# Attention output kept in four interleaved runs of tokens, and the token order put back on the way out of PSUM

## The chip, the cores and the metric

The kernel runs on one core of a Trainium2 chip. The metric is the time of one execution on the device in microseconds; lower is better. Before the change it takes 340.39 us (median of 3 runs, 340.26 to 340.43).

## The reference

Three stages follow each other on 1152 tokens (2 batches of 576), each of width 512. The kernel computes all of it in float32, most matmuls as three products of high and low parts (`float32r`).

```python
# 1. linear attention, 8 heads of 64, 128 random features, per batch
phi(x) = exp(h - max(h)) / sqrt(m),  h = x @ omega.T - |x|^2 / 2
num = phi(q) @ (phi(k).T @ v);  den = phi(q) @ sum(phi(k)) + 1e-6
x = (num / den) as [1152 tokens, 512]
# 2. MLP
h = x @ w_in                     # [512, 2048]
x = (h * sigmoid(1.702 * h)) @ w_out
# 3. top-1 mixture of 8 experts with a capacity of 288 tokens each
e = argmax(x @ w_gate);  gate = softmax(x @ w_gate)[e]
out = gate * (relu(x @ w1[e]) @ w2[e])     # tokens past the capacity stay 0
```

## The kernel before

**Attention.** Rows of q, k and v are loaded so that partition n holds the tokens 4n to 4n+3 of a head (n below 128; `JF` is 4), 512 of a batch's 576 tokens; the other 64 tokens are loaded apart, two heads one above the other. Everything up to the normalised result is done for each j = 0 to 3 by itself: the matmul with the features (`pj`), the exponentials on ACT (`kp`, `qp`), phi(k).T @ v (`kvp`), the transposes of phi(q) (`t`, copied to `qt`), the numerators (`nps`) and the division on DVE (`xr`). `do_X(b, p, u)` then turns `xr` by four transposes into a PSUM bank `xps` of 128 x 512, feature by (j, n). `x_out` copies the bank twice: ACT rounds it into `x_hi` (line 398), DVE subtracts that from the bank into `x_lo` (line 399). `x_hi` and `x_lo` have the shape [128, 4, 1152], feature by feature chunk and token, in the order of the tokens; token 4n+j is the element 4n+j, so the bank's unbroken elements go to every fourth place. There are 8 such outputs. `do_Xm(b, p)` does the same for the 64 other tokens, with a bank of 2 chunks x 64 tokens whose order is already that of the tokens; there are 4 of these.

**PSUM.** Small results take the banks of `mbank`, which hands out two single banks, L and M, by turns (later M alone). The next user of a bank waits until the last reader of the one before is done. `t`, `nps`, `xps`, and the gate's `wt_ps`, `wg_ps` and `wp_ps` share them. `tp` and `h_ps` have two banks, `pj` and the MLP's `y` three and one.

**First MLP.** The tokens are taken in four groups G of 288 (`GS`), 16 blocks m of 128 hidden features. `do_h(G, m)` makes 12 matmuls of 288 columns (4 feature chunks c, three products each, `mm3`, lines 98 to 100): weights stationary, `x_hi` or `x_lo` of the group's tokens moving. ACT computes the activation, and `do_y` adds up four output banks of 288 tokens. Groups 0, 1 and 3 are interleaved, with a lag of 3 and 5 blocks; group 2 comes after them. For groups 1 and 3 no second product is made here, only the logits (`do_lg`, with weights folded by `do_wt`, `do_wg` and `do_wp`), since their tokens are outside the two experts computed ahead. After the last block of groups 0 and 2 `do_y` copies the four banks over `x_hi` and `x_lo` (lines 645 and 646). The weights are decoded block by block on DVE (lines 236 to 242), ACT (`win0h` and so on, line 248) and POOL (`win0l`, line 249), in four tiles of [128, 4, 512] for each matrix, where block m of `w_in` takes columns 128(m % 4) on of each chunk.

**Gate and experts.** `do_logits(G)` multiplies `x_hi` and `x_lo` with the gate for G = 0 and 2, copies the result from PSUM (`lgy`, line 726; for G = 1 and 3 `do_lg` has made `lgt`, line 659), transposes it by 96 tokens, and DVE adds the parts (`lg`, line 739). `do_pos` counts tokens of each expert in order of the tokens. `pick_slot` picks an expert for group 0 and one for group 2; its weights are loaded (`eraw`) and split (`eh`, `el`). `do_h2` and `do_y2` are the expert's two products, 8 blocks each, 12 matmuls of 288 columns a block. `do_z_out` copies the four result banks to `z`, by turns on DVE and ACT (lines 879 and 881); `z_rows` transposes 96 tokens at a time, and the rows are masked, scaled and written out. Loops for tokens that are left follow; with these inputs they are not entered.

**Order of the work.** Attention is written out as 40 steps with lags; what remains of it after the last step is put, with a higher priority, between the first slots of the MLP, which begin at about 87 us. The layer that lays out the instructions then gives each engine its own queue, in order, and puts in the waits. In the time between 87 and 110 us the queue of TensorE therefore holds matmuls of attention and of the MLP by turns.

Of the kernel before, what the change touches and what calls it, by code (L numbers as in the profile page):

```python
# [35 lines left out]
def linear_attention__moe__top1_moe_kernel(  # L36
# [14 lines left out]
    nc = tc.nc  # L51
# [12 lines left out]
    TJ = GS // TT  # L64
    JF = S // 128
    SF = JF * 128
    NU = 18
    NP = NG * E
    VW = D + 1
# [123 lines left out]

    x_hi = xp.tile([128, KD, NT], F32R, name="x_hi")
    x_lo = xp.tile([128, KD, NT], F32R, name="x_lo")
    W = {}
    def w_pair(pool, kind, i):
        t = [pool.tile([128, 4, 512], F32R, tag=f"w{kind}{i}{s}", name=f"w{kind}{i}{s}") for s in "hl"]  # L200
# [200 lines left out]
    def do_X(b, p, u):  # L401

        xr = xrs.pop((b, p, u))
        ps = mbank("xps")
        for j in range(JF):
            nc.tensor.transpose(ps[:, j * 128:(j + 1) * 128], xr[:, j], ident)
        hi, lo = (t[:, 2 * p + u, b * S:b * S + SF].rearrange("p (n j) -> p j n", j=JF)
                  for t in (x_hi, x_lo))
        x_out(hi, lo, ps.rearrange("p (j n) -> p j n", j=JF))

    def do_Xm(b, p):
        ps = mbank("xps")
        for u in range(2):
            nc.tensor.matmul(ps[:, u * 64:(u + 1) * 64], xms[p][:, u], fold, start=True, stop=True)
        hi, lo = (t[:, 2 * p:2 * p + 2, b * S + SF:(b + 1) * S] for t in (x_hi, x_lo))
        x_out(hi, lo, ps[:, :128].rearrange("p (u n) -> p u n", u=2))

    npre = len(P["dec"])
    wseq = [(kd, m) for m in range(NF) for kd in ("in", "out")]
# [189 lines left out]
        return [gp.tile([128, GS], F32R, tag=tag, name=tag, bufs=2) for tag in ("ghi", "glo")]  # L609

    def do_h(G, m, full=False):
        tk = slice(G * GS, G * GS + GS)
        hi, lo = w_in(m)
        ps = bank("A", "h_ps")
        for c in range(KD):
            mm3(ps[:, :GS], hi[:, c], lo[:, c], x_hi[:, c, tk], x_lo[:, c, tk],
                c == 0, c == KD - 1)
        if G % 2 and not full:
            g1 = gp.tile([128, GS], F32, tag="g1", name="g1", bufs=5)
            mark["a"] = nc.scalar.activation(g1, ps[:, :GS], ACTF.Gelu_apprx_sigmoid)  # L620
            gs[G, m] = g1
            return
        ghi, glo = parts_tile(G != 0)
        nc.scalar.activation(ghi, ps[:, :GS], ACTF.Gelu_apprx_sigmoid)  # L624
        g32 = gp.tile([128, GS], F32, tag="g1", name="g32", bufs=5)
        mark["a"] = nc.scalar.activation(g32, ps[:, :GS], ACTF.Gelu_apprx_sigmoid)  # L626
        mark["v"] = nc.vector.tensor_tensor(glo, g32, ghi.bitcast(F32), ALU.subtract)  # L627
        gs[G, m] = (ghi, glo)
# [4 lines left out]
    def do_y(G, m):  # L633
        if m == 0:
            yps[G] = y_banks()
        ghi, glo = gs.pop((G, m))
        hi, lo = w_out(m)
        for c in range(KD):
            dc = slice(c * 128, c * 128 + 128)
            mm3(yps[G][c][:, :GS], hi[:, dc], lo[:, dc], ghi, glo, m == 0, m == NF - 1)  # L640
        if m == NF - 1:
            for c in range(KD):
                sl = (slice(None), c, slice(G * GS, G * GS + GS))
                y = yps[G][c][:, :GS]
                nc.scalar.copy(x_hi[sl], y)
                nc.vector.tensor_tensor(x_lo[sl], y, x_hi[sl].bitcast(F32), ALU.subtract)

    def do_lg(G, m):


        i = G - 1 + m % 2
        if i in lgq:
            run_lg()
        lgq[i] = (m, gs.pop((G, m)))
        if len(lgq) == 4 or (G, m) == (3, NF - 1):
            run_lg()
        if (G, m) == (3, NF - 1):
            held_t.append(gp.tile([128, GS], F32, tag="g1", name="lgt", bufs=5))
            nc.scalar.copy(held_t[0], held.pop()[:, :GS])

    lgq, held_t, now = {}, [], [0]

# [53 lines left out]
    def do_logits(G):  # L716
        if G % 2 == 0:
            ps = mbank("lg_ps")
            for c in range(KD):
                tk = slice(G * GS, G * GS + GS)  # L720
                nc.tensor.matmul(ps[:2 * E, :GS], wg[:, c].rearrange("p a e -> p (a e)"), x_hi[:, c, tk],
                                 start=(c == 0), stop=False)
                nc.tensor.matmul(ps[:E, :GS], wg[:, c, 0], x_lo[:, c, tk],
                                 start=False, stop=(c == KD - 1))
            t = gp.tile([2 * E, GS], F32, tag="g1", name="lgy", bufs=5)
            nc.scalar.copy(t, ps[:2 * E, :GS])
            n = 2 * E
        else:
            n = 64 if G == 1 else 128
            t = held_t[0]  # L730
# [124 lines left out]
    def do_h2(key, m, wt, tok):  # L855
# [1 line left out]
        hi, lo = wt[m // 4]  # L857
        fc = slice((m % 4) * 128, (m % 4) * 128 + 128)
        for c in range(KD):
            mm3(ps[:, :GS], hi[:, c, fc], lo[:, c, fc], x_hi[:, c, tok], x_lo[:, c, tok],  # L860
                c == 0, c == KD - 1)
        hhi, hlo = parts_tile(True)
        nc.scalar.activation(hhi, ps[:, :GS], ACTF.Relu)
# [12 lines left out]
    def do_z_out(key, z):  # L876
        for c in range(KD):
            if c % 2:
                nc.scalar.copy(z[:, c], zps[key][c][:, :GS])
            else:  # L880
                nc.vector.tensor_copy(z[:, c], zps[key][c][:, :GS])

    def z_rows(z, j):
        ps = mbank("zt_ps")
# [106 lines left out]
    slot(NSL + NF2 + 3, lambda: slot_rows(0, 1))  # L991
    slot(NSL + NF2 + 4, lambda: slot_rows(0, 2))

    def tokens(G):
        return slice(G * GS, (G + 1) * GS)

    for n in range(NSL + 2 * NF2 + 2):
        now[0] = n
        if n < NSL:
# [23 lines left out]
    with tc.If(n_left > 0):  # L1023
# [23 lines left out]
        with tc.For_i(0, n_left):  # L1047
# [19 lines left out]
                split_e(wt, i, "x")  # L1067
            for m in range(NF2 + 1):
                if m < NF2:
                    do_h2("x", m, wt, ds(gv * GS, GS))  # L1070
                if m:
                    do_y2("x", m - 1, wt)
            z, base = scratch(0)
# [38 lines left out]
```

## Time and profile before

| | |
|---|---|
| median of 3 runs | 340.39 us (340.26 to 340.43) |
| the profiled execution | 339.27 us, of it 337.5 from the first to the last instruction (the span) |
| mean granted TensorE clock | 0.996 |
| TensorE busy | 318.7 us, 94% |
| VectorE (DVE) busy | 182.9 us, 54% |
| ScalarE (ACT) busy | 172.4 us, 51% |
| GpSimd (POOL) busy | 60.4 us, 18% |

A group of instructions is written as line, engine, operation, output<-inputs, shapes and count, then busy us and mean ns of one, then the idle time of the engine just before them and what ended it. PE is TensorE's matmul. The ends of matmuls are modelled: matmuls are pipelined, and one row lasts longer than the distance to the next. In the chain of waits each piece is start us, length us and what.

### The profile page before, as it was taken

How to read it: one execution, taken by the hardware profiler on the slowest of the kernel's cores; microseconds unless marked ns; L12 is line 12 of the kernel's file. 1: busy time of each engine (PE TensorE's matmuls, PEld its weight loads, DVE VectorE, ACT ScalarE, POOL GpSimd, SP SyncE). 2: the span in 40 equal slices, each digit the busy share in tenths (PEclk: the TensorE clock that was granted, in tenths of full speed). 3: DMA queues.
4: the chain of work that ended last, by engine and by line, in shares of the span. 5: the costliest groups of instructions: out<-in, count | busy, mean ns of one | idle time of the engine just before them, and what ended most of it. 6: DMA issues, size and time to landing. Idle time of an engine off the chain costs nothing.

```text
span 337.5 us, 6635 instructions
## 1 busy us (share of the span) xinstructions
PE 318.7 (94%) x2569; PEld 304.3 (90%) x2569; DVE 182.9 (54%) x438; ACT 172.4 (51%) x445; POOL 60.4 (18%) x83
## 2 busy tenths in 40 slices
PE   5999999989997999999999999999999999999991
PEld 4999998889896999999999999989999999998990
DVE  5678797887578775444446403117434123568322
ACT  2788888879834454444444434233634233165312
POOL 3110311122003444443443410000000001010000
PEclk9999999999999999999999999999999999999998
DMA  6999541401030545435441000523400000383202
GB/s 173 296 328 271 166 134 62 127 15 50 0 105 25 186 130 172 151 122 170 124 135 64 0 2 0 156 95 94 135 23 0 2 1 2 110 271 119 72 0 80
DMA packets 29079, 35.19 MB, mean 104 GB/s; under 512 B 5360, under 2 KB 23792, under 8 KB 29040
## 3 DMA queue, kind: packets, MB, share of 16 engines
q1 hardware_dynamic: 29040, 34.69, 33.0%
q8 instruction: 22, 0.36, 0.5%
q14 instruction: 17, 0.14, 0.1%
HBM read 32.33 MB, written 2.36 MB: 103 GB/s over the span
## 4 chain that ended last, share of the span: by engine, by line
PE 82%; ACT 6%; DVE 5%; DMA 4%; issue 1%; POOL 0%; SPq 0%; ACTq 0%; DVEq 0%
PE h_ps L98 12%; PE h_ps L99 12%; PE h_ps L100 12%; PE y L98 7%; PE y L100 7%; PE y L99 7%; PE kvp L339 4%; PE nps L364 3%; DMA eraw<-in_moe_w_dram 3%; PE tp L282 2%; PE pj L98 2%; ACT x_hi L398 2%; PE t L353 2%; PE pj L99 2%; PE pj L100 2%; PE wt_ps L492 2%
## 5 line engine op out<-in xcount | busy, mean ns | idle before, releaser
L627 DVE TENSOR_TENSOR glo<-g,ghi 128x288 fp32r<-128x288 f32 x27 | 12.9, 478 | 38.7 <-ACT g L626 38.7
L236 DVE TENSOR_SCALAR wf<-wraw 128x512 int32<-128x512 int32 x32 | 16.2, 512 | 26.9 <-POOL win2l L249 10.8
L620 ACT ACTIVATE g<-h_ps 128x288 f32<-128x288 f32 x32 | 13.2, 412 | 29.4 <-PE h_ps L100 24.5
L308 DVE TENSOR_REDUCE nb<-pj 128x4 f32<-128x512 f32 (+1 forms) x40 | 25.1, 631 | 3.9 <-PE pj L100 3.5
L851 DVE TENSOR_TENSOR el<-eraw,eh 128x1024 fp32r<-128x1024 f32 x16 | 19.5, 1222 | 12.0 <-ACT eh L850 12.0
L98 PE MATMUL pj<-om_hi,xh 128*128 128x256 f32 x72 | 24.6, 341 | 1.0 <-ACT qp L321 1.0
L242 DVE SCALAR_TENSOR_TENSOR wf<-wraw,wf 128x512 int32<-128x512 int32 x32 | 25.0, 784 | 0.5
L624 ACT ACTIVATE ghi<-h_ps 128x288 fp32r<-128x288 f32 x27 | 11.1, 412 | 24.5 <-PE h_ps L100 23.9
L850 ACT CAST eh<-eraw 128x1024 fp32r<-128x1024 f32 x16 | 16.7, 1049 | 13.4 <-PE h_ps L99 7.3
L321 ACT ACTIVATE qp<-pj,nb 128x128 f32<-128x128 f32 x72 | 21.8, 389 | 0.7 <-DVE nb L308 0.5
L239 DVE SCALAR_TENSOR_TENSOR wf<-wraw,wf 128x512 int32<-128x512 int32 x32 | 21.9, 691 | 0.2
L99 PE MATMUL pj<-om_lo,xh 128*128 128x256 f32 x72 | 21.7, 301 | 0.0
L321 ACT ACTIVATE kp<-pj,nb 128x128 f32<-128x128 f32 x72 | 21.6, 394 | 0.0
L100 PE MATMUL pj<-om_hi,xl 128*128 128x256 f32 x72 | 21.4, 298 | 0.0
L285 ACT CAST xh<-tp 128x256 fp32r<-128x256 f32 (+1 forms) x40 | 14.7, 369 | 11.7 <-PE tp L282 11.7
L98 PE MATMUL h_ps<-x_hi,win0h 128*128 128x288 f32 x64 | 20.1, 314 | 0.0
L100 PE MATMUL h_ps<-x_hi,win0l 128*128 128x288 f32 x64 | 19.2, 300 | 0.5 <-POOL win0l L249 0.5
L339 PE MATMUL kvp<-vt,kp 128*128 128x65 f32 (+1 forms) x144 | 19.7, 269 | 0.0
L98 PE MATMUL h_ps<-x_hi,win3h 128*128 128x288 f32 x64 | 19.6, 306 | 0.0
L98 PE MATMUL h_ps<-x_hi,win2h 128*128 128x288 f32 x64 | 19.6, 306 | 0.0
L98 PE MATMUL h_ps<-x_hi,win1h 128*128 128x288 f32 x64 | 19.4, 303 | 0.0
L98 PE MATMUL h_ps<-x_hi,eh 128*128 128x288 f32 x64 | 19.2, 300 | 0.0
(246 smaller groups left out, 1080.5 us busy)
## 6 DMA issues: line engine op xcount, KB each, us to landing
wraw<-in_moe_w_in_dram SPq DMA_DIRECT2D x16, 512.0 KB, 4.3
wraw<-in_moe_w_out_dram SPq DMA_DIRECT2D x16, 512.0 KB, 3.6
eraw<-in_moe_w_dram SPq DMA_DIRECT2D x16, 512.0 KB, 4.7
qk_raw<-in_v_dram SPq DMA_DIRECT2D x4, 512.0 KB, 5.2
qk_raw<-in_q_dram SPq DMA_DIRECT2D x4, 512.0 KB, 5.2
qk_raw<-in_k_dram SPq DMA_DIRECT2D x3, 512.0 KB, 5.1
out_dram<-zer SPq DMA_DIRECT2D x2, 576.0 KB, 6.3
out_dram<-base SPq DMA_DIRECT2D x6, 192.0 KB, 3.0
```

What stands on the lines that cost most here:

```text
L98: nc.tensor.matmul(o, lh, rh, start=start, stop=False)
L99: nc.tensor.matmul(o, lh, rl, start=False, stop=False)
L100: nc.tensor.matmul(o, ll, rh, start=False, stop=stop)
L236: nc.vector.tensor_scalar(f, high, 3, 0x3FFFFFF8, ALU.logical_shift_left, ALU.bitwise_and)
L239: nc.vector.scalar_tensor_tensor(f, high, -0x40000000, f, ALU.bitwise_and, ALU.bitwise_or)
L242: nc.vector.scalar_tensor_tensor(f, low, 29, f, ALU.logical_shift_right, ALU.bitwise_or)
L285: nc.scalar.copy(xh[:, :n], tp[:, :n])
L308: mark["M", s] = nc.vector.tensor_reduce(nb[:, :nj], pj[:, :nj * M].rearrange("p (a m) -> p a m", m=M), AX, ALU.min)
L321: nc.scalar.activation(t[:, i], pj[:, i * M:(i + 1) * M], ACTF.Exp, bias=nb[:, i:i + 1], scale=-1.0)
L339: nc.tensor.matmul(ps[:, o:o + n], kp[:, i], vts[p][:, u, c0:c0 + n], start=(f == 0), stop=(f == NU - 1))
L850: nc.scalar.copy(hi, tv)
L851: nc.vector.tensor_tensor(lo, tv, hi.bitcast(F32), ALU.subtract)
```

## The change

`x_hi` and `x_lo` become [128, 4, 4, 288]: token 4i+j lies at (j, i). `do_X` now writes four runs of 128 elements. `do_Xm` writes its 64 tokens to 16 places in each of four runs, so that its inner step is 288 elements. All matmuls on a group of tokens read four runs of 72 in place of one of 288; their results have the order (j, i) in PSUM. `do_y` writes its banks back to `x_hi` and `x_lo` in that order. Where a result leaves PSUM for good (`lgy`, `lgt`, `z`), the copy reads PSUM in steps of 72 elements and writes the tokens in their own order; nothing behind these copies changes. The number of instructions is the same, and no DMA is touched.

```diff
+    NI = NT // JF
+    GI = GS // JF
+    BI = S // JF
...
-    x_hi = xp.tile([128, KD, NT], F32R, name="x_hi")
-    x_lo = xp.tile([128, KD, NT], F32R, name="x_lo")
+    def tokens(G):
+        return slice(G * GI, (G + 1) * GI)
+    def in_order(t):
+        return t.rearrange("p (j i) -> p i j", j=JF)
+    def rows_of(t):
+        return t.rearrange("p (i j) -> p i j", j=JF)
+    x_hi = xp.tile([128, KD, JF, NI], F32R, name="x_hi")
+    x_lo = xp.tile([128, KD, JF, NI], F32R, name="x_lo")
...
@@ do_X
-        hi, lo = (t[:, 2 * p + u, b * S:b * S + SF].rearrange("p (n j) -> p j n", j=JF)
-                  for t in (x_hi, x_lo))
+        hi, lo = (t[:, 2 * p + u, :, b * BI:b * BI + 128] for t in (x_hi, x_lo))
@@ do_Xm
-        hi, lo = (t[:, 2 * p:2 * p + 2, b * S + SF:(b + 1) * S] for t in (x_hi, x_lo))
-        x_out(hi, lo, ps[:, :128].rearrange("p (u n) -> p u n", u=2))
+        hi, lo = (t[:, 2 * p:2 * p + 2, :, b * BI + 128:(b + 1) * BI].rearrange("p u j i -> p u i j")
+                  for t in (x_hi, x_lo))
+        x_out(hi, lo, ps[:, :128].rearrange("p (u i j) -> p u i j", u=2, j=JF))
@@ do_h (do_h2 and do_logits alike)
-            mm3(ps[:, :GS], hi[:, c], lo[:, c], x_hi[:, c, tk], x_lo[:, c, tk],
+            mm3(ps[:, :GS], hi[:, c], lo[:, c], x_hi[:, c, :, tk], x_lo[:, c, :, tk],
@@ do_y
-                sl = (slice(None), c, slice(G * GS, G * GS + GS))
-                y = yps[G][c][:, :GS]
+                sl = (slice(None), c, slice(None), tokens(G))
+                y = yps[G][c][:, :GS].rearrange("p (j i) -> p j i", j=JF)
@@ do_lg
-            nc.scalar.copy(held_t[0], held.pop()[:, :GS])
+            nc.scalar.copy(rows_of(held_t[0]), in_order(held.pop()[:, :GS]))
@@ do_logits
-            nc.scalar.copy(t, ps[:2 * E, :GS])
+            nc.scalar.copy(rows_of(t), in_order(ps[:2 * E, :GS]))
@@ do_z_out
-                nc.scalar.copy(z[:, c], zps[key][c][:, :GS])
+                nc.scalar.copy(rows_of(z[:, c]), in_order(zps[key][c][:, :GS]))
             else:
-                nc.vector.tensor_copy(z[:, c], zps[key][c][:, :GS])
+                nc.vector.tensor_copy(rows_of(z[:, c]), in_order(zps[key][c][:, :GS]))
```

## Rows read from the trace of the kernel before

**Rows 1.** The page: engines' busy time, and the chain that ended last by engine

```profile
PE 318.7 (94%) x2569; PEld 304.3 (90%) x2569; DVE 182.9 (54%) x438; ACT 172.4 (51%) x445; POOL 60.4 (18%) x83
...
PE 82%; ACT 6%; DVE 5%; DMA 4%; issue 1%; POOL 0%; SPq 0%; ACTq 0%; DVEq 0%
```

**Rows 2.** TensorE by stretch: length, busy (instructions), granted clock, DMA; one sum of five

```profile
87.00:90.00 3.00, 2.26 (x20) 1.00 0.00 0
sum 15.00, PE 13.09; mean PE 2.62
...
65.50:71.00 5.50, 3.83 (x41) 1.00 0.24 84
101.50:108.00 6.50, 4.11 (x29) 1.00 0.03 13
30.00:110.00 80.00, 73.75 (x618) 1.00 0.27 84
110.00:304.00 194.00, 193.97 (x1571) 1.00 0.30 93
270.00:280.00 10.00, 10.00 (x77) 1.00 0.00 1
```

**Rows 3.** The chain of waits from 33 to 88 us, pieces of two outputs

```profile
33.64 1.09 ACT x_hi L398
...
34.76 1.10 DVE x_lo L399
...
86.55 1.11 ACT x_hi L398
```

**Rows 4.** TensorE's instructions in order of time, about 35 us

```profile
35.13 0.36 PE L98 MATMUL pj<-om_hi,xh 128*128 128x256 f32 x1
35.92 0.66 PE L353 MATMUL t<-ident,qp 128*128 128x128 f32 x4 [0.42 <-DVE den L382]
```

**Rows 5.** Groups of instructions on DVE and ACT, by shape

```profile
L308 DVE TENSOR_REDUCE nb<-pj 128x4 f32<-128x512 f32 x32 | 21.8, 684 | 1.7 <-PE pj L100 1.3
...
L355 ACT COPY qt<-t 128x512 f32<-128x512 f32 x16 | 9.5, 594 | 4.1 <-PE t L353 3.8
...
L399 DVE TENSOR_TENSOR x_lo<-xps,x_hi 128x512 fp32r<-128x512 f32 x8 | 8.8, 1095 | 7.1 <-ACT x_hi L398 7.0
L398 ACT CAST x_hi<-xps 128x512 fp32r<-128x512 f32 x8 | 8.7, 1089 | 2.9 <-PE xps L406 2.8
...
L384 DVE TENSOR_TENSOR xr<-nps,den 128x256 f32<-128x256 f32 x16 | 6.7, 418 | 0.1
...
L308 DVE TENSOR_REDUCE nb<-pj 128x2 f32<-128x256 f32 x8 | 3.4, 420 | 2.2 <-PE pj L100 2.2
...
L248 ACT CAST win1h<-wf 128x512 fp32r<-128x512 f32 x4 | 2.5, 626 | 2.4 <-DVE wf L242 2.4
...
L881 DVE COPY z<-y 128x288 f32<-128x288 f32 x4 | 1.8, 455 | 3.0 <-PE y L100 3.0
...
L879 ACT COPY z<-y 128x288 f32<-128x288 f32 x4 | 1.5, 399 | 3.9 <-PE y L100 3.9
...
L398 ACT CAST x_hi<-xps 128x128 fp32r<-128x128 f32 x4 | 1.1, 266 | 4.8 <-PE xps L414 4.8
L739 DVE TENSOR_REDUCE lg<-lgr_ps 96x24 f32<-96x48 f32 x4 | 0.8, 202 | 6.0 <-PE lgr_ps L733 6.0
```

**Rows 6.** The chain of waits from 65 to 107 us, pieces of two stretches

```profile
65.48 1.00 ACT x_hi L398
...
67.84 1.44 DVE wf L236
...
103.58 1.29 POOL win0l L249
...
104.90 1.51 DVE wf L236
```

**Rows 7.** The chain of waits about 306 us

```profile
306.51 0.47 DVE z L881
```

More of the change, by code (lines that the diff above doesn't have):

```diff
@@ L611, in do_h @@
     def do_h(G, m, full=False):
-        tk = slice(G * GS, G * GS + GS)
+        tk = tokens(G)
         hi, lo = w_in(m)
@@ L719, in do_logits @@
             for c in range(KD):
-                tk = slice(G * GS, G * GS + GS)
-                nc.tensor.matmul(ps[:2 * E, :GS], wg[:, c].rearrange("p a e -> p (a e)"), x_hi[:, c, tk],
+                tk = tokens(G)
+                nc.tensor.matmul(ps[:2 * E, :GS], wg[:, c].rearrange("p a e -> p (a e)"), x_hi[:, c, :, tk],
                                  start=(c == 0), stop=False)
-                nc.tensor.matmul(ps[:E, :GS], wg[:, c, 0], x_lo[:, c, tk],
+                nc.tensor.matmul(ps[:E, :GS], wg[:, c, 0], x_lo[:, c, :, tk],
                                  start=False, stop=(c == KD - 1))
             t = gp.tile([2 * E, GS], F32, tag="g1", name="lgy", bufs=5)
-            nc.scalar.copy(t, ps[:2 * E, :GS])
+            nc.scalar.copy(rows_of(t), in_order(ps[:2 * E, :GS]))
             n = 2 * E
@@ L859, in do_h2 @@
         for c in range(KD):
-            mm3(ps[:, :GS], hi[:, c, fc], lo[:, c, fc], x_hi[:, c, tok], x_lo[:, c, tok],
+            mm3(ps[:, :GS], hi[:, c, fc], lo[:, c, fc], x_hi[:, c, :, tok], x_lo[:, c, :, tok],
                 c == 0, c == KD - 1)
@@ L992, in linear_attention__moe__top1_moe_kernel @@
     slot(NSL + NF2 + 4, lambda: slot_rows(0, 2))
-    def tokens(G):
-        return slice(G * GS, (G + 1) * GS)
     for n in range(NSL + 2 * NF2 + 2):
@@ L1069, in linear_attention__moe__top1_moe_kernel @@
                 if m < NF2:
-                    do_h2("x", m, wt, ds(gv * GS, GS))
+                    do_h2("x", m, wt, ds(gv * GI, GI))
                 if m:
```

## The prediction, made before the result was known

> **What bounds the kernel now.** I read the page first, then the time line of TensorE by stage, then groups of instructions by shape, then the chain of waits. The page says that TensorE is busy for 94% of the span and holds 82% of the chain that ended last, with ACT 6% and DVE 5% beside it [rows 1]. So nothing counts that does not move TensorE. The stretches show where it could move: from 110 to 304 us it is busy for 193.97 of 194 us, while from 30 to 110 us, where attention ends and the first MLP sets in, it is busy for 73.75 of 80, so 6.25 us of idleness lie there [rows 2]. Nearly all of that lies right behind the eight outputs of attention (`do_X`): five short stretches that each follow one of them hold 15.00 - 13.09 = 1.91 us, the stretch from 65.5 to 71 us holds 1.67 and the one from 101.5 to 108 us 2.39, together 5.97 of the 6.25 [rows 2]. The clock is granted in full in every one of these rows, so it is no term.
>
> The chain of waits shows the mechanism at 33.64 us: ACT writes `x_hi` for 1.09 us, DVE then writes `x_lo` for 1.10, and only then do four transposes start, since `x_lo` was the last reader of their PSUM bank [rows 3]. On TensorE the transposes start at 35.92, 0.79 us after the matmul before them (the row names `den`, which DVE starts as `x_lo` ends) [rows 4], where matmuls of that shape start about 0.12 us apart. Seven of the eight wide outputs stand in the chain, five of them with both copies, the first at 33.64 and the last of these five at 86.55 [rows 3].
>
> **The change part by part.**
>
> *The eight wide outputs.* Each copies 128x512 from PSUM into every fourth element of `x_hi` (ACT) and `x_lo` (DVE); after it, in four unbroken runs of 128. The strided copies take 1089 and 1095 ns; the same number of elements written unbroken takes ACT 594 ns (`qt`), and a DVE pass over 128x512 of PSUM 684 ns [rows 5]. That runs cost nothing of themselves is seen in `xr`: 256 elements in four runs of 64 take 418 ns, and an unbroken DVE pass over 256 takes 420 [rows 5]. So ACT saves 1089 - 594 = 495 ns and DVE 1095 - 684 = 411, say 0.88 us (0.91 less a little, as the reduction writes little and a subtraction writes all) on each hand-over from bank to bank.
>
> What of it TensorE gets: after the five simple outputs the idle time in front of the waiting instruction is 1.91 us in all, on average 0.38, at most 0.74 (the last, from 87 to 90 us) [rows 2], which is less than 0.88; all of it goes. It is a lower bound, as matmul ends are modelled: at 35.92 the idle time is written as 0.42, while 0.79 - 0.12 = 0.67 us passed without a start [rows 4]. With 0.2 added for each, and no more than 0.88 for one, the five give up to 2.8.
>
> From 65.5 to 71 us the wait is longer: ACT's `x_hi` at 65.48 holds up ACT's next exponentials (TensorE waits for their bank), `x_lo` holds up DVE's decode at 67.84 with its 1.44 us [rows 6], and behind that `xl` and `xm`, for which TensorE waits again. Both queues move up by the saving, so 0.88 of the 1.67 goes; the slow decode instruction remains. From 101.5 to 108 us two outputs stand close together on ACT, and behind them in ACT's queue `win0h`, behind that POOL's `win0l`, DVE's decode, and last a narrow output's matmuls. Two ACT savings, 2 x 0.495 = 0.99 us, reach POOL; its 1.29 us and DVE's 1.51 stay [rows 6]. So 0.98 of the 2.39 goes.
>
> Sum of the gain: 1.91 + 0.88 + 0.98 = 3.77 us (up to 2.8 + 1.86 = 4.7; if the two long stretches give only half, 1.91 + 0.93 = 2.8). What is late next: the other reader of the two small PSUM banks, and in the long stretches POOL. From 110 us TensorE is full, so a stage that begins earlier ends earlier.
>
> *The four narrow outputs* (`do_Xm`) lose: 128 elements went out unbroken in 266 ns [rows 5], and now each goes to another place. By the wide rows a scattered element costs (1089 - 594) / 512 = 0.97 ns more, so 0.12 us on ACT and as much on DVE. Two of the four lie beside full TensorE time; bounds for all: 0 to 0.24 x 4 = 1.0 us. I take 0, since no TensorE wait ends on a narrow copy.
>
> *The MLP matmuls.* The 4 x 16 x 12 + 2 x 8 x 12 = 960 matmuls of `h_ps` and the 16 of the logits now read their moving operand in four runs of 72. No row of this trace has a moving operand in more than one run. The bounds: below, a gain is excluded, since the operand is unbroken today. The nearest row is `xr`, where four runs cost DVE nothing. [...] One scattered element for each break, 3 x 0.97 ns, would be 2.8 us. I take 0, as by `xr`. [...]
>
> *MLP results into `x_hi`* (eight pairs, four runs of 72): 0, as by `xr`.
>
> *Order put back on leaving PSUM.* `lgy`, `lgt` and the eight copies `z` now read PSUM in steps of 72 elements and write unbroken. DVE has a row for that: the logit reduction reads 48 elements, none beside the next, in 202 ns; the two reductions over 512 and 256 give 684 - 420 = 264 ns per 256, 1.03 an element, so 420 - 208 x 1.03 = 206 ns for 48 [rows 5]. The steps cost nothing there. ACT has no such row. Below nothing is excluded, the write being unbroken before and after. Upper bound: 0.97 ns for each element as in the strided writes, 288 x 0.97 = 0.28 us a copy. On the path would be `lgy`, which is ahead of the second expert's load, two `z` of DVE in the first expert's results (the second of them at 306.51 [rows 7]), and the last `z` of ACT, for which the final transposes wait: 4 x 0.28 = 1.1 us. I take 0 for DVE and 0.15 for the two ACT copies together. [...]
>
> *Dependencies.* The tokens of different groups now lie between each other in `x_hi`. If the layer that places waits saw a tile's stretch from first to last element as one, `h_ps` would wait for outputs of other tokens. The decoded weights already lie like that (four runs of 128 in one tile, each read and written by another step), and `win1h` waits only for DVE, never for a matmul [rows 5]. So 0. No DMA is added, moved or changed, and nothing on SP's or POOL's queue.
>
> **Sum.** -3.77 + 0.15 = -3.6 us. The profiled execution took 339.27 us (span 337.5), so it would take 335.7; the median of the runs shown is 340.39, 1.1 above it, so I say 336.8 us for the median. About 0.2%, 0.7 us, is what a measurement of this kernel can tell from no change.
>
> **Rivals.**
>
> 1. *The matmuls pay for their runs* (the slower side). Place: every `h_ps` matmul from 87 us on, where TensorE has no slack [rows 2]. The point of balance is 3.6 / 976 = 3.7 ns for each, 2.8% of a step; from 4.4 ns it is measurably slower. [...] For it: nothing else in this trace reads so. Against it: `xr`, and that a break is no new instruction. 0.12.
>
> 2. *The waits are replaced.* The instruction that waited for `x_lo` finds the other bank, an exponential or POOL's 1.3 us in its way, or the instructions come out in another order on the queues, and under 0.7 us arrives: about 340.0. For it: ACT and DVE are busy for most of this stage, and two of the seven stretches have POOL or a slow decode in them [rows 6]. Against it: in five places the chain names both copies [rows 3]. 0.09.
>
> 3. *Stepped PSUM reads are dear on both engines:* 1.1 us instead of 0.15, so 337.7. For it only the size of the strided writes; against it the logit row [rows 5]. [...] 0.09.
>
> **How the numbers follow.** The forecast, gain of 1.5 to 5 us, has 0.70 and a range of its own of 335.3 to 338.9. Rival 3 is faster too. Of rival 2 half is faster by a little, of rival 1 a small part ends level. Faster: 0.70 + 0.09 = 0.79, less 0.02 for what may be lost in both, so 0.77; same 0.10; slower 0.13. The range runs from the upper sum, 340.4 - 4.7 - 0.5 for savings in other gaps, 335.2, to 340.3, where rival 2 ends; the matmul case lies outside.
>
> **What would show it.** The wide `x_hi` copy at about 600 ns and `x_lo` at about 700; if these stay above 1000 ns, the whole forecast falls. TensorE's idle time from 30 to 110 us at about 2.5 us in place of 6.25, with the transposes after the first output waiting for nothing. 77 `h_ps` and `y` matmuls in 10 us of the dense stage, as now; 74 or fewer would be rival 1. `z` on ACT at 399 ns and on DVE at 455 as now [rows 5], or about 680 and 735 for rival 3. A matmul that waits for `x_hi` of another group of tokens would show that the dependencies went wrong.

## The result, and the profile after

The kernel after took 334.49 us (median of 4 runs, 334.21 to 334.96) against 340.32 for the kernel before (4 runs, 339.16 to 340.43): a ratio of 0.984, interval 0.9803 to 0.9877. The forecast was 336.8 us with a range from 335.2 to 340.3. The direction was right; the time came out 2.3 us under the forecast and 0.7 us under the range. Over all runs of this study the kernel after has a median of 334.96 (15 executions) and the kernel before one of 339.81 (44), 4.85 us apart. The two profiled executions are 5.06 us apart: 334.21 with a span of 332.4, and 339.27 with 337.5.

The page of the kernel after, first the engines and then the chain that ended last [rows 1]:

```profile
PE 317.0 (95%) x2569; PEld 303.7 (91%) x2569; DVE 178.7 (54%) x438; ACT 169.4 (51%) x445; POOL 60.3 (18%) x83
...
PE 86%; DMA 5%; ACT 3%; DVE 2%; SPq 1%; issue 1%; POOL 0%; ACTq 0%; DVEq 0%
```

The numbers of instructions are the same. ACT and DVE have lost about half of their share of the chain (6% to 3%, 5% to 2%), and TensorE has taken most of it (82% to 86%). The instructions of every queue stand in the same order in both traces, so nothing was laid out anew. TensorE by stretch (length, busy time and instructions, granted clock, DMA) [rows 2]:

```profile
30.00:110.00 80.00, 77.66 (x658) 1.00 0.31 96
270.00:280.00 10.00, 10.00 (x78) 1.00 0.01 2
```

The idleness between 30 and 110 us fell from 6.25 to 2.34 us (the prediction said about 2.5), and the dense stage is as dense as it was, 78 matmuls in 10 us against 77. Groups of instructions by shape (busy us, mean ns of one, then the idle time before) [rows 5]:

```profile
L411 DVE TENSOR_TENSOR x_lo<-xps,x_hi 128x512 fp32r<-128x512 f32 x8 | 5.5, 692 | 3.6 <-ACT x_hi L410 3.3
L410 ACT CAST x_hi<-xps 128x512 fp32r<-128x512 f32 x8 | 4.7, 591 | 2.9 <-PE xps L418 2.8
...
L893 DVE COPY z<-y 128x288 f32<-128x288 f32 x4 | 1.8, 453 | 3.0 <-PE y L103 3.0
L410 ACT CAST x_hi<-xps 128x128 fp32r<-128x128 f32 x4 | 1.6, 393 | 4.6 <-PE xps L425 4.5
L411 DVE TENSOR_TENSOR x_lo<-xps,x_hi 128x128 fp32r<-128x128 f32 x4 | 1.5, 387 | 0.7 <-ACT x_hi L410 0.7
...
L891 ACT COPY z<-y 128x288 f32<-128x288 f32 x4 | 1.5, 400 | 4.0 <-PE y L103 4.0
```

The wide copies went from 1089 and 1095 ns to 591 and 692, the narrow ones rose from 266 to 393 on ACT (387 on DVE, where step_psum below has the unbroken 280), and the copies that now read PSUM in steps of 72 elements (`z`, 453 and 400 ns) cost what the unbroken ones cost (455 and 399). The matmuls that read four runs of 72 cost nothing more either; here one group of the kernel before and the same one after:

```profile
L98 PE MATMUL h_ps<-x_hi,win1h 128*128 128x288 f32 x64 | 19.4, 303 | 0.0
```

```profile
L101 PE MATMUL h_ps<-x_hi,win1h 128*128 128x288 f32 x64 | 19.4, 303 | 0.0
```

**Where the time came from.** Idle time on TensorE depends on modelled ends; starts do not. So the best ruler is the time from one wide output's four transposes (`xps`, line 406 before, 418 after) to the next one's, and from the eighth to the first transposes of `lgt` in the gate (`lgr_ps`; those of group 0's `lgy` come about 20 us earlier), behind which the distance of the two traces hardly changes. As an example the fourth, the fifth and the gate, on the time line (start, length, engine, line, operation), before and then after:

```profile
64.69 0.60 PE L406 MATMUL xps<-ident,xr 128*128 128x128 f32 x4
78.86 0.60 PE L406 MATMUL xps<-ident,xr 128*128 128x128 f32 x4
...
227.57 0.37 PE L733 MATMUL lgr_ps<-ident,lgt 64*96 64x64 f32 x3
```

```profile
63.13 0.60 PE L418 MATMUL xps<-ident,xr 128*128 128x128 f32 x4
75.73 0.60 PE L418 MATMUL xps<-ident,xr 128*128 128x128 f32 x4
...
222.19 0.37 PE L745 MATMUL lgr_ps<-ident,lgt 64*96 64x64 f32 x3
```

The intervals, in us, each from two such starts (the kernels other than these two are described below; three more of them have their intervals where they are described):

| kernel | 1 to 2 | 2 to 3 | 3 to 4 | 4 to 5 | 5 to 6 | 6 to 7 | 7 to 8 | 8 to gate |
|---|---|---|---|---|---|---|---|---|
| before | 8.00 | 14.10 | 9.58 | 14.17 | 6.95 | 14.03 | 0.84 | 126.89 |
| after | 7.36 | 13.68 | 9.25 | 12.60 | 6.31 | 13.27 | 0.84 | 126.04 |
| after_again | 7.36 | 13.68 | 9.25 | 12.60 | 6.31 | 13.25 | 0.84 | 127.46 |
| after_b | 7.36 | 13.67 | 9.26 | 12.60 | 6.32 | 13.27 | 0.83 | 126.05 |
| step_psum | 7.36 | 13.68 | 9.26 | 12.59 | 6.31 | 13.16 | 0.84 | 126.04 |
| both_slow | 7.96 | 14.13 | 9.58 | 14.15 | 6.91 | 14.10 | 0.84 | 128.25 |
| act_slow | 7.58 | 13.88 | 9.36 | 12.96 | 6.55 | 13.69 | 0.83 | 126.86 |
| dve_slow | 7.51 | 13.75 | 9.25 | 12.62 | 6.43 | 13.56 | 0.83 | 126.08 |
| late_wf | 7.36 | 13.67 | 9.26 | 13.26 | 6.32 | 13.25 | 0.84 | 127.36 |
| late_wf_b | 7.36 | 13.69 | 9.25 | 13.25 | 6.32 | 13.26 | 0.84 | 127.38 |

An interval of one kernel repeats within 0.02 us from execution to execution, but for the last one, of which more below. Before less after: 0.64, 0.42, 0.33, 1.57, 0.64, 0.76, 0 and 0.85, in all 5.21 us. The intervals 1 to 2, 2 to 3, 3 to 4, 5 to 6 and 6 to 7 are the prediction's five simple outputs: 2.79 us. The interval 4 to 5 holds its stretch from 65.5 to 71 us: 1.57. The last one holds its stretch from 101.5 to 108 us: 0.85. The first output is 0.17 us earlier, which is within the spread of its start between executions (more below); with it the gate is 5.38 us earlier; 0.3 of that is lost again by the end, and the spans differ by 5.1.

What is left of TensorE's waits in the kernel after (total us, times, longest):

```profile
PE xps L425 <- DVE xm L406: 1.1, 1, 1.1
...
PE h_ps L103 <- POOL win0l L261: 0.6, 1, 0.6
```

None of them ends on a wide copy any more.

**What the interval 4 to 5 shows.** All engines' time line, first of the kernel before:

```profile
67.71 1.28 POOL L249 TENSOR_TENSOR win0l<-wf,win0h 128x512 fp32r<-128x512 f32 x1 [6.28 <-ACT win0h L248]
67.84 1.44 DVE L236 TENSOR_SCALAR wf<-wraw 128x512 int32<-128x512 int32 x1
...
69.72 0.58 DVE L394 TENSOR_TENSOR xm<-nps,den 64x128 f32<-64x128 f32 x2
69.86 0.33 PE L282 MATMUL tp<-ident,qk_raw 128*128 128x128 f32 x1 [0.58 <-DVE xl L292]
...
70.45 0.64 PE L502 MATMUL wg_ps<-wt,wg_f 128*32 128x128 f32 x16 [0.26 <-DVE xm L394]
```

and then of the kernel after:

```profile
64.44 0.69 DVE L411 TENSOR_TENSOR x_lo<-xps,x_hi 128x512 fp32r<-128x512 f32 x1 [1.26 <-ACT x_hi L410]
65.39 0.43 DVE L248 TENSOR_SCALAR wf<-wraw 128x512 int32<-128x512 int32 x1
65.78 1.28 POOL L261 TENSOR_TENSOR win0l<-wf,win0h 128x512 fp32r<-128x512 f32 x1 [6.17 <-ACT win0h L260]
...
66.27 0.58 DVE L406 TENSOR_TENSOR xm<-nps,den 64x128 f32<-64x128 f32 x2
...
67.32 0.65 PE L514 MATMUL wg_ps<-wt,wg_f 128*32 128x128 f32 x16
```

The reader is to look at two starts. Before, POOL's `win0l` begins at 67.71 and DVE's decode `wf` at 67.84, 0.13 us behind it, and the decode takes 1.44 us: it ends at 69.28, 0.29 after POOL (67.71 + 1.28 = 68.99). After, the decode begins at 65.39, 0.39 ahead of POOL, and takes 0.43 us. The "slow decode instruction" of the prediction was not slow by itself; it stood behind POOL. Of the 32 decodes of this shape the median takes 0.43 us in both traces. How the one instruction holds up the other no run shows. What the trace shows is that the decode ends only behind POOL's instruction, 0.29 us behind it; that this is less than the decode's own 0.43 us is not explained by any run.

One more decode turns over between the two traces. At 46.60 us before, it takes 1.08 us behind POOL's `wout0l` of 46.12; after, it starts with `wout0l` at 44.89 and takes 0.43, and POOL 1.55. TensorE does not gain by it: from its `kvp` matmuls beside the decode to its next transposes 0.67 us pass in both (46.65 to 47.32, 45.42 to 46.09).

### The profile page after: what moved, and what is told of

Its sections match the earlier page's. It is cut to its first block, busy times and chain, and to the rows that moved or that the text cites. A ratio compares the mean times of both kernels' runs of the same rounds, so it can differ in the third digit from the quotient of the medians.

```text
span 332.4 us, 6635 instructions
## 1 busy us (share of the span) xinstructions
PE 317.0 (95%) x2569; PEld 303.7 (91%) x2569; DVE 178.7 (54%) x438; ACT 169.4 (51%) x445; POOL 60.3 (18%) x83
## 3 DMA queue, kind: packets, MB, share of 16 engines
HBM read 32.33 MB, written 2.36 MB: 104 GB/s over the span
## 4 chain that ended last, share of the span: by engine, by line
PE 86%; DMA 5%; ACT 3%; DVE 2%; SPq 1%; issue 1%; POOL 0%; ACTq 0%; DVEq 0%
PE h_ps L101 13%; PE h_ps L102 12%; PE h_ps L103 12%; PE y L101 7%; PE y L102 7%; PE y L103 7%; PE kvp L351 4%; PE nps L376 4%; DMA eraw<-in_moe_w_dram 3%; PE pj L101 2%; PE t L365 2%; PE pj L102 2%; PE pj L103 2%; PE tp L294 2%; PE wt_ps L504 2%; DMA qk_raw<-in_k_dram 2%
## 5 line engine op out<-in xcount | busy, mean ns | idle before, releaser
L248 DVE TENSOR_SCALAR wf<-wraw 128x512 int32<-128x512 int32 x32 | 14.5, 458 | 28.2 <-POOL win2l L261 10.8
```

Of the source, the lines that this page charges most:

```text
L248: nc.vector.tensor_scalar(f, high, 3, 0x3FFFFFF8, ALU.logical_shift_left, ALU.bitwise_and)
```

## The experiments

Two theories stood after the comparison. The first: the copies' length does it all, in two ways, as shorter hand-overs (the 0.88 us a piece of the prediction) and, at one place that TensorE waits for, as an earlier start of the decode that takes it out of POOL's way. The rival: some of the 5 us comes from elsewhere in the change, the new token order (matmuls, dependencies), and the copies give only the predicted 3.8.

**The same kernel again** (after_again, after_b): the kernel after, unchanged.

> The changed kernel once more, as the measure for the other runs. Theory (queue and collision): what the prediction missed is real. Time 334.5 us, 5.5 us under the kernel before; in this second trace the decode instruction that took 1.44 us at 67.84 us takes about 0.43 us again, since it starts ahead of POOL's win0l. Rival (jitter): the first trace was a lucky one; here the decode takes over 1 us, or the difference is about 3.8 us as in the prediction's sum.

Measured: 335.25 us (334.47 to 335.62), ratio 0.9874 (0.985 to 0.9898) against a before of 339.57. The decode took 0.43 us again, at 65.07, with POOL's `win0l` at 65.45.

> The kernel after, unchanged, for a comparison with the late decode within one set of runs. Theory (a sum of stalls, 5.1 to 5.8 us): 334.5 to 335.3 us against a before near 339.8; the decode behind the gating sum (wf, 128x512 int32, near 65 us) takes 0.43 us again and starts ahead of GpSimd's win0l. Second theory, on the spread between executions of one kernel: if TensorE's granted clock falls behind the stall at 99 to 102 us in some executions and not in others, this trace shows either 1.00 in all of 102 to 106 us, or 0.5 there and everything behind it about 1 us later.

Measured: 334.85 us (334.44 to 336.34), ratio 0.9849 (0.982 to 0.9877) against a before of 340.33. So the distance lies between 4.3 and 5.8 us, by the set of runs. The table says why: up to the eighth output the three executions agree in each interval within 0.02 us, and after_again is 1.41 us longer in the last one. Its TensorE there (length, busy, granted clock, DMA), and the same of the kernel after below it:

```profile
98.00:100.00 2.00, 1.43 (x11) 1.00 0.00 0
100.00:102.00 2.00, 0.96 (x7) 0.88 0.00 0
102.00:104.00 2.00, 2.00 (x11) 0.50 0.06 13
104.00:106.00 2.00, 2.00 (x14) 0.77 0.79 249
```

```profile
98.00:100.00 2.00, 1.44 (x11) 1.00 0.00 0
100.00:102.00 2.00, 0.95 (x8) 1.00 0.00 0
102.00:104.00 2.00, 2.00 (x18) 1.00 0.00 0
104.00:106.00 2.00, 2.00 (x17) 1.00 0.79 243
```

After the same idleness (1.43 and 0.96 us busy of 2, against 1.44 and 0.95) the granted clock falls from 1.00 to 0.50 in one execution and stays at 1.00 in the other. It makes 11 matmul records in 2 us instead of 18. Among the profiled executions of this study the fall is in after_again, both_slow, late_wf and late_wf_b, each time behind this same stall, and these are the rows of the table with 1.3 to 1.4 us more in the last interval than their like. This, and the start of the first output (32.51 to 33.58 us in the three executions), is what these traces show of the spread between executions that the timings below carry. What decides whether the clock falls was not found.

**The copies' part alone** (step_psum): the kernel before, whole, with the two wide copies reading PSUM in steps and writing in the order of the tokens, unbroken.

```diff
-        hi, lo = (t[:, 2 * p + u, b * S:b * S + SF].rearrange("p (n j) -> p j n", j=JF)
+        hi, lo = (t[:, 2 * p + u, b * S:b * S + SF].rearrange("p (n j) -> p n j", j=JF)
                   for t in (x_hi, x_lo))
-        x_out(hi, lo, ps.rearrange("p (j n) -> p j n", j=JF))
+        x_out(hi, lo, ps.rearrange("p (j n) -> p n j", j=JF))
```

> The kernel before with one edit: the wide copies write x_hi and x_lo unbroken in the order of the tokens and read PSUM in steps of 128 elements instead. No matmul reads in runs, no result is put back in order. Theory (only the strided SBUF write was dear, a stepped PSUM read is free): wide copies 590 to 700 ns, narrow ones 266 and 278 as before, time within 0.5 us of the changed kernel, 334.0 to 335.0 us. Rival (PSUM steps are dear in long copies): copies near 1.09 us and 340 us. Rival (the layout itself gives part of the gain): 336 us or more with fast copies.

Measured: 334.6 us (333.71 to 336.68), ratio 0.987 (0.984 to 0.99), beside 335.25 for the kernel after in the same set. Its copies by shape:

```profile
L399 DVE TENSOR_TENSOR x_lo<-xps,x_hi 128x512 fp32r<-128x512 f32 x8 | 5.5, 692 | 3.7 <-ACT x_hi L398 3.3
L398 ACT CAST x_hi<-xps 128x512 fp32r<-128x512 f32 x8 | 4.7, 592 | 2.9 <-PE xps L406 2.8
...
L399 DVE TENSOR_TENSOR x_lo<-xps,x_hi 128x128 fp32r<-128x128 f32 x4 | 1.1, 280 | 0.6 <-ACT x_hi L398 0.6
L398 ACT CAST x_hi<-xps 128x128 fp32r<-128x128 f32 x4 | 1.1, 267 | 4.6 <-PE xps L414 4.5
```

Two lines do all that the change does: the step of 128 elements between one read of PSUM and the next costs ACT and DVE nothing (592 and 692 ns, as with unbroken reads in the kernel after), where the step of four on the side of the write had cost 0.4 to 0.5 us (1095 and 1089 ns). The narrow copies stay at 267 and 280 ns, and the interval 6 to 7 is 0.11 us shorter than in the kernel after, the only one in which the two differ by more than 0.02. Neither the new token order nor the work to undo it was needed.

**The new order with slow copies** (both_slow, act_slow, dve_slow): the kernel after, all of it, but the wide copies written element by element, each 288 places from the last; both, only ACT's, only DVE's. Here is both_slow; act_slow and dve_slow do it to the first or the second of the two instructions.

```diff
-        hi, lo = (t[:, 2 * p + u, :, b * BI:b * BI + 128] for t in (x_hi, x_lo))
-        x_out(hi, lo, ps.rearrange("p (j n) -> p j n", j=JF))
+        nc.scalar.copy(x_hi[:, 2 * p + u, :, b * BI:b * BI + 128].rearrange("p j n -> p n j"),
+                       ps.rearrange("p (j n) -> p n j", j=JF))
+        nc.vector.tensor_tensor(x_lo[:, 2 * p + u, :, b * BI:b * BI + 128].rearrange("p j n -> p n j"),
+                                ps.rearrange("p (j n) -> p n j", j=JF),
+                                x_hi[:, 2 * p + u, :, b * BI:b * BI + 128].rearrange("p j n -> p n j").bitcast(F32),
+                                ALU.subtract)
```

> [...] Theory (all of the gain is the wide copies): copies about 1.1 us, time back at 340.3 us, within 0.7 us. Rival (runs in the matmuls or the layout gain or cost something): a time away from that of the kernel before by the size of it; at 3.7 ns a matmul it would be 344 us.

Measured: 339.47 us (338.39 to 341.54), ratio 0.9994 (0.9976 to 1.0011). With copies of 1072 and 1081 ns the whole change is worth nothing, and every interval up to the eighth output is the one of before within 0.07 us. Its time line from 66 us:

```profile
66.74 1.07 DVE L420 TENSOR_TENSOR x_lo<-xps,x_hi 128x512 fp32r<-128x512 f32 x1 [1.65 <-ACT x_hi L419]
67.96 1.28 POOL L261 TENSOR_TENSOR win0l<-wf,win0h 128x512 fp32r<-128x512 f32 x1 [6.28 <-ACT win0h L260]
68.06 1.47 DVE L248 TENSOR_SCALAR wf<-wraw 128x512 int32<-128x512 int32 x1
```

The decode is behind POOL again, and slow again. The rival falls with these two runs: the copies are sufficient (step_psum) and necessary (both_slow).

> The changed kernel with only ACT's wide copy slow (1.09 us), DVE's in runs (0.7). Theory: the five simple stalls come back by what is over after 0.4 us of DVE's saving, about 1.0 us in all; the stretch at 65 us loses 0.5 us, but POOL's win0l moves back with ACT, so the decode still starts ahead of it and stays at 0.43 us; the stretch at 100 us loses 1.0 us. About 337.0 us. Rival (no collision theory, the savings simply add): half of the gain lost, 337.4 us, without a telling decode row.

Measured: 336.87 us (336.36 to 338.22), ratio 0.9934 (0.9909 to 0.996). The rival's 337.4 is within the spread, so the time does not choose; the decode took 0.43 us, as the theory said, and against the kernel after the five simple intervals lose 1.19 us (1.0 expected), 4 to 5 loses 0.36 (0.5) and the last 0.82 (1.0).

> The changed kernel with only DVE's wide copy slow (1.09 us), ACT's in runs (0.6). Theory: the simple stalls come back by about 0.7 us; the decode behind x_lo at 65 us now starts 0.4 us later, after POOL's win0l has begun, and takes about 1.4 us, so 1.0 us more comes back there, with up to 0.4 at 100 us: 336.5 to 337.0 us. Rival (the decode's 1.44 us belongs to itself and not to POOL): the decode stays at 0.43 us and the time is about 335.5 us.

Measured: 335.3 us (333.77 to 335.72), ratio 0.9848 (0.9814 to 0.9882). The decode of 1.4 us, on which the 336.5 to 337.0 rested, did not come:

```profile
65.19 1.05 DVE L420 TENSOR_TENSOR x_lo<-xps,x_hi 128x512 fp32r<-128x512 f32 x1 [1.26 <-ACT x_hi L419]
66.49 0.43 DVE L248 TENSOR_SCALAR wf<-wraw 128x512 int32<-128x512 int32 x1
66.53 1.54 POOL L261 TENSOR_TENSOR win0l<-wf,win0h 128x512 fp32r<-128x512 f32 x1 [6.07 <-ACT win0h L260]
```

The decode begins 0.04 us ahead of POOL and is fast; this time POOL pays, 1.54 us instead of 1.28. In the kernel after the decode leads POOL by 0.39 us, and the slower copy takes back 0.36 of it (1.05 us against 0.69): the expectation took for certain what was nearly a tie. It is the order of two starts that decides, not their distance. Over the 13 traces of this study, 23 decodes of this shape start 0.03 to 0.49 us behind a POOL subtraction of 128x512, and every one ends 0.28 to 0.29 us after it (1.06 to 1.53 us long); 20 start with one or ahead of it, by up to 0.39 us, and every one takes 0.42 to 0.43. In sum over the intervals act_slow loses 2.36 us against the kernel after and dve_slow 0.68, together 3.0; both_slow loses 5.2, when the 1.36 us are left out by which its last interval, with the fall of the clock, is longer than that of before. The parts do not add, since ACT's copy and DVE's stand one behind the other: each alone is partly taken up by the idleness that the other has left.

**The collision alone** (late_wf, late_wf_b): the kernel after, with the first operation of that decode issued behind the reciprocal of the gating sum on DVE, so that POOL has begun.

```diff
-            nc.vector.reciprocal(d[:, 0:2], d[:, 0:2])
+            mark["r"] = nc.vector.reciprocal(d[:, 0:2], d[:, 0:2])
...
-                at(s + d + 1, fs[d])
+                at(s + d + 1, paced(fs[d], "r") if (s, d) == (DEC_AT[-1], 0) else fs[d])
```

> The changed kernel with one instruction moved on DVE's queue: the decode near 65 us is issued behind the reciprocal, so that it starts while POOL's win0l runs; order and work of the other engines are the same. Theory (collision of DVE and POOL): the decode takes 1.0 to 1.5 us instead of 0.43, the small transposes' input xm comes about 1 us later, and the time rises by 0.5 to 1.0 us, to 335.0 to 335.5 us. Rival (its 1.44 us had another cause): 0.43 us and no change beyond 0.2 us.

Measured: 335.09 us (334.02 to 336.56), ratio 0.9847 (0.9814 to 0.988), in a set of runs without the kernel after. So it was timed again beside it:

> The kernel after, with the sixth decode's first operation issued behind the reciprocal of the gating sum, so that GpSimd's win0l has begun when it starts. If the collision on 512-element instructions is worth what the stretch 65 to 70 us gained beyond the prediction (1.55 against 0.88), this kernel is 0.6 to 1.0 us slower than the kernel after in the same set of runs, near 335.5 to 336.0, with wf at 1.4 to 1.5 us. If the decode's delay is hidden later, the medians differ by less than 0.2 us although wf takes 1.4 to 1.5 us.

Measured: 335.76 us (334.05 to 336.32), ratio 0.9856 (0.9828 to 0.9885), beside 334.85 and 0.9849 (0.982 to 0.9877) for the kernel after. The medians are 0.9 us apart, but the intervals of the ratios lie almost upon each other, so the timing alone does not settle it. The trace does:

```profile
64.43 0.69 DVE L411 TENSOR_TENSOR x_lo<-xps,x_hi 128x512 fp32r<-128x512 f32 x1 [1.25 <-ACT x_hi L410]
...
65.39 0.42 DVE L304 TENSOR_TENSOR xl<-tp,xh 128x256 fp32r<-128x256 f32 x1
...
65.77 1.27 POOL L261 TENSOR_TENSOR win0l<-wf,win0h 128x512 fp32r<-128x512 f32 x1 [6.17 <-ACT win0h L260]
65.80 1.52 DVE L248 TENSOR_SCALAR wf<-wraw 128x512 int32<-128x512 int32 x1
...
67.25 0.58 DVE L406 TENSOR_TENSOR xm<-nps,den 64x128 f32<-64x128 f32 x2
...
67.97 0.64 PE L514 MATMUL wg_ps<-wt,wg_f 128*32 128x128 f32 x16 [0.58 <-DVE xm L406]
```

`x_lo` starts where it starts in the kernel after (64.43 and 64.44). The decode, 0.03 us behind POOL, takes 1.52 us; `xm` is behind it, and the gate's matmuls start at 67.97 instead of 67.32, waiting for it. The interval 4 to 5 is 13.25 and 13.26 us in the two executions, 12.60 in three of the kernel after: in this order of DVE's queue the collision costs TensorE 0.65 us. The later start alone would not: the same instructions stand between `x_lo` and `xm` in both kernels, and with 0.43 us the decode would end at 65.80 + 0.43 = 66.23, while `xm` starts at 66.27 in the kernel after. No other interval gives the 0.65 back: those up to the eighth output are unchanged, and the last (127.36 and 127.38 us, with the fall of the clock) is within 0.1 us of after_again's 127.46, which has the fall too. All 12 executions of the late decode have a median of 335.53 us, 0.57 over the 15 of the kernel after.

The rest, 14.17 - 13.25 = 0.92 us, is not simply the copies' part. In late_wf `xl` has come ahead of the decode; in the kernel before it is behind it, and TensorE waits for it too (0.58 us, at 69.86). An estimate from the rows of before, with its order kept: with a decode of 0.43 us in place of 1.44 `xm` would start 1.01 us earlier, at 68.71, and the gate's matmuls 0.73 us behind it, as they do there, at 69.44 instead of 70.45. TensorE's own work would allow 69.32: its `kvp` matmuls start at 68.50, and 0.82 us pass from these to the gate's in the kernel after. By this the collision is worth about 1.0 us and the copies about 0.56. The two kernels in which one copy is slow and the decode fast point the same way: in this interval act_slow loses 0.36 us and dve_slow 0.02, while both_slow, with the slow decode, loses 1.55. So of the 1.57 us the collision has between 0.65 and about 1.0, by the order on DVE; no run removes it from the kernel before with nothing else changed.

**The matmuls' runs, made as bad as can be** (scatter_mm): the kernel after, where all `h_ps` and logit matmuls read their tokens in the old order, each element 288 places from the one before; the results, then in the order of the tokens, leave PSUM unbroken.

```diff
+    def one(t, c, tk):
+        return t[:, c, :, tk].rearrange("p j i -> p i j")
...
-            mm3(ps[:, :GS], hi[:, c], lo[:, c], x_hi[:, c, :, tk], x_lo[:, c, :, tk],
+            mm3(ps[:, :GS], hi[:, c], lo[:, c], one(x_hi, c, tk), one(x_lo, c, tk),
```

> The changed kernel with the moving operand of every h_ps and logit matmul read in the order of the tokens, so each of its 288 elements lies 288 places from the last, and results leave PSUM unbroken. The prediction's slower rival taken to its end. If TensorE pays for a break as ACT and DVE do for a scattered write (0.97 ns an element), a matmul would take 0.13 + 0.28 us and the time would rise by some 270 us. If its reads do not care for the place of an element: 334.5 us, within 0.5. Four runs of 72 cost nothing in the trace, so I lean to a cost between, seen only with scattered elements.

Measured: 352.89 us (352.3 to 353.48), ratio 1.0384 (1.0342 to 1.0427). Against the 334.96 of the kernel after, 17.9 us for 976 matmuls, 18 ns for one of 288 columns. In its groups those with a scattered moving operand have grown, and those of the second product, whose operand is unbroken, have not:

```profile
L102 PE MATMUL h_ps<-x_lo,win1h 128*128 128x288 f32 x64 | 20.3, 318 | 0.0
...
L101 PE MATMUL y<-ghi,wout1h 128*128 128x288 f32 x24 | 7.1, 296 | 0.0
```

In the kernel after these are 295 and 295 ns. So the prediction's first rival names something real, which four runs of 72 do not touch: step_psum, with unbroken operands, and the kernel after both take 126.04 us from the eighth output to the gate.

**Towards a better version** (early_before, best_1). The stall at 100 us is left in the kernel after: ACT's `win0h` stands behind the two last outputs, POOL's `win0l` and `wout0l` behind that, DVE's decode collides with `wout0l` (1.49 us at 99.52, 0.07 behind it), and `xm` is behind the decode. The edit hands the ACT and POOL part of the first two decodes of the MLP out one slot earlier: early_before does it to the kernel before, best_1 to step_psum.

```diff
-    def decode_slot(n):
+    def decode_slot(n, dd=P["dd"]):
...
-        slot(n + P["dd"], paced(fs[3], "a"))
+        slot(n + dd, paced(fs[3], "a"))
...
-        slot(n, lambda n=n: decode_slot(n))
+        slot(n, lambda n=n, i=i: decode_slot(n, 1 if i < 2 else P["dd"]))
```

> The kernel before with PSUM read in steps (as in the run step_psum) and ACT's and POOL's part of the first two decodes in the MLP one slot earlier, so that win0h goes into ACT's idle 2.5 us ahead of the last two outputs. Theory: POOL's win0l and wout0l then run earlier, the decode near 100 us neither waits for them nor collides, and the two TensorE gaps there of 0.7 and 1.2 us shrink: 1.0 to 1.8 us under step_psum, about 333 us. Rival (another wait takes their place, since the order on TensorE changes too): within 0.5 us of step_psum.

Measured: 333.27 us (332.23 to 333.92), ratio 0.9795 (0.9764 to 0.9825), the fastest version of the study: 1.2 us under the first median of the kernel after, 1.7 under that of its 15 executions, 1.3 under step_psum, which was timed in another set of runs. Its time line at the last outputs:

```profile
94.49 1.28 POOL L249 TENSOR_TENSOR win0l<-wf,win0h 128x512 fp32r<-128x512 f32 x1 [17.85 <-ACT win0h L248]
...
95.73 1.29 POOL L249 TENSOR_TENSOR wout0l<-wf,wout0h 128x512 fp32r<-128x512 f32 x1
...
95.80 1.49 DVE L236 TENSOR_SCALAR wf<-wraw 128x512 int32<-128x512 int32 x1 [0.55 <-POOL win0l L249]
...
97.99 0.63 PE L406 MATMUL xps<-ident,xr 128*128 128x128 f32 x4 [0.99 <-DVE xr L384]
```

POOL is 3.7 us earlier than in the kernel after (`win0l` at 98.22 there), but the collision has moved along with it: the decode starts 0.07 us behind `wout0l` and takes 1.49 us, and now the eighth output's transposes wait behind it. So the expected decode without a collision did not come, though the expected time did. From the seventh output to the gate best_1 takes 2.25 + 123.45 = 125.70 us and step_psum 126.88: 1.18 gained.

> The kernel before, its broken writes kept, with the decodes of the first two MLPs on ACT and GpSimd one slot earlier. GpSimd's win0l is then far from the decode that it collided with. Theory (the collision cost about 0.9 us of the 5.1, and an early decode gives 1.3 us at 100 us, as it did beside the unbroken writes): wf near 68 us takes 0.43 us with the wide copies still at 1.09 us, and the time is 1.5 to 2.5 us under the before of these runs, near 337.5. Rival (only the copies' length counts, the collision was beside the path): about 338.5, the 1.3 us alone.

Measured: 338.18 us (337.06 to 338.66), ratio 0.9935 (0.9911 to 0.9958), 2.15 us under its before of 340.33 and 1.6 under that of all 44 executions. The expectation of a fast decode near 68 us failed: it took 1.45 us there, behind a `win0l` of 67.42, since that `win0l` belongs to a decode of the time before the MLP's slots, which the edit leaves where it is. From the seventh output to the gate it takes 126.35 us against 127.73 before, 1.38 gained; the rest of the 2.15 is not in its intervals. So this edit is worth 1.2 to 1.4 us with either kind of copy, and it does not remove a collision.

## Why the prediction was wrong

*What held.* The wide copies at 591 and 692 ns (594 and 684 were said). Four runs of 72 on TensorE at nothing (303 ns in both traces for the group shown above); the first rival is out at this length of run, by the dense stage (78 matmuls in 10 us against 77, a start every 0.13 us), by both_slow (339.47 us beside a before of 339.57) and by step_psum's equal last interval (126.04 us). Stepped reads of PSUM at nothing (`z` 453 and 400 ns, against 455 and 399 unbroken): the third rival is out, and the 0.15 us set aside for `z` was too much by all of it. In step_psum each of 512 reads is 128 elements or more from the last, and the copies take 592 and 692 ns, beside 591 and 692 with unbroken reads. The 1.1 us was the prediction's own upper bound, and the time of one such copy came out unchanged. The narrow copies at 0.13 and 0.11 us more, where 0.12 was estimated; they cost the path 0.11 us once (after against step_psum), where 0 was said. No wait for another group's tokens came up, and no order of instructions changed.

*What failed: three terms.* The sum of gains was 3.77 us; the intervals give 5.21, and the missing 1.44 falls apart so:

| term | predicted | measured |
|---|---|---|
| five simple outputs | 1.91 | 2.79 |
| stretch from 65.5 to 71 us | 0.88 | 1.57 (of it the collision 0.65 to about 1.0) |
| stretch from 101.5 to 108 us | 0.98 | 0.85 |

First, the size: "the five give up to 2.8" stood in the prediction as the upper end, and 1.91 was taken. The text itself had the reason why 1.91 could not be the value, "it is a lower bound, as matmul ends are modelled", with one place worked out: 0.42 us of idleness where 0.67 passed without a start [rows 4]. The right reading was the distance of starts. The upper end came out, 2.79, and not by luck: the five places have 0.42, 0.21, 0.11, 0.42 and 0.74 us of idleness, and with 0.2 more for each the first four are within 0.02 us of the measured 0.64, 0.42, 0.33 and 0.64; at the fifth TensorE moves up by 0.89 us at once, and the narrow copy takes 0.11 back.

Second, the step that failed as a mechanism: "Both queues move up by the saving, so 0.88 of the 1.67 goes; the slow decode instruction remains." The decode did not remain slow. The 1.44 us in [rows 6] was taken for the instruction's own length, though its median over the kernel is 0.43; it was a wait behind POOL's `win0l`, lost by 0.13 us at the start. Counted from the start of the fourth output's transposes, DVE's decode moved from 3.15 to 2.26 us, by both savings, and POOL's `win0l` only from 3.02 to 2.65, since of the two copies ACT's alone is ahead of it; the order of the two starts turned over, and 1.57 us went instead of 0.88. Whether 0.88 was the right size for the shorter copies by themselves stays open (0.92 by late_wf, about 0.56 by the estimate). The prediction saw the same pattern at 104.9 us (1.51 us behind `wout0l`), and there it was right that it stays: DVE waits there for POOL's `win0l` (the row in best_1 names it), so it starts when POOL's next one does.

Third, the range. Its low end lay 4.7 + 0.5 under the old median, and the profiled executions are 5.06 apart, so what the mechanism gave would just have stayed inside it. Of the 2.3 us by which the forecast was off, 1.5 lie between the profiled executions (335.7 forecast, 334.21 measured) and 0.8 in the step from the profiled execution to the median: 1.1 us was added, since the three runs shown of before stood high (340.26 to 340.43; 44 executions have 339.81, 0.5 over the profiled one), while the kernel after stood at 0.3 over its own in the first four runs. The offset changes with the set of runs and is no constant of the kernel: counted from 339.81, the same low end would be 334.6, and 334.96, the median of all 15 executions of the kernel after, would lie above it.

The second rival (waits replaced by others) was right in kind at one place, the stall at 100 us, where 0.85 us was gained of the 0.98 said, and the wait of 1.1 us for `xm`, behind the decode and POOL, is what is late next; its time of 340.0 was not.

## What to carry to other kernels

Where a copy out of PSUM has to change the order of elements, put the step on the read and leave the write unbroken: here that cost nothing (592 and 692 ns with the step on the read, 1089 and 1095 with it on the write), took two lines, and made a new layout superfluous. Size a stall on TensorE by the distance between starts, and an instruction by its group's median: the decode that took three times as long as its like (1.44 us against 0.43) had waited, and the trace shows for whom if one looks at which of DVE and POOL started first. Here such a wait hung on the order of two starts, so a saving upstream removed it whole (interval 4 to 5, the decode at 0.43 us) and an earlier slot moved it along (best_1, the decode at 1.49).

## What the hardware showed that was not expected

- A DVE decode of 128x512 int32 that starts 0.03 to 0.13 us behind a POOL subtraction of 128x512 takes 1.44 to 1.53 us instead of 0.43, and at any lag up to 0.49 us it ends 0.28 to 0.29 us after it; one that starts 0.04 us ahead takes 0.43, and POOL 1.54 instead of 1.28.
- Reads of PSUM in steps of 72 or 128 elements cost ACT and DVE nothing (400 and 453 ns over 288 elements in steps of 72, against 399 and 455 unbroken; 592 and 692 over 512 in steps of 128, against 591 and 692); writes to SBUF in steps do: 1089 and 1095 ns over 512 for a step of 4 elements, 1072 and 1081 for one of 288.
- TensorE reads its moving operand in four runs of 72 at no cost (303 ns for one of `win1h`'s group before and after; 77 and 78 matmuls in 10 us of the dense stage), and element by element, 288 places apart, for 18 ns more per matmul of 288 columns (17.9 us over 976).
- TensorE's granted clock fell from 1.00 to 0.50 (0.88, 0.50 and 0.77 in three stretches of 2 us) behind one stall in one execution of the kernel after and not in two others, at a price of 1.4 us; the falls in both_slow and late_wf cost 1.3 to 1.4 us likewise.
